# One scratch operand of a float64 split moves from SBUF to a PSUM bank

## The chip, the cores and the metric
One Trainium2 chip, one of its cores. The metric is the device time of one execution in microseconds (us). Engines: TensorE multiplies matrices, VectorE and ScalarE work elementwise on SBUF and PSUM, GpSimd works elementwise on SBUF and issues the indexed transfers, SyncE issues the other transfers. In the profile they are PE (PEld for its weight loads), DVE, ACT, POOL and SP; a name with a trailing q (SPq) is the engine's instruction queue.

## The reference
Three layers, one after the other: a gated recurrent attention (4 x 8 heads, 768 positions, 40 wide), a mixture of 8 experts with one expert per token (3072 tokens of 320), and a dense layer with a rational function between its two products.

```
for t in range(S): C = f*C + i*v k^T;  n = f*n + i*k;  y[t] = sigmoid(o) * (C q) / max(|n q|, 1)
idx = argmax(xn @ en.T / tau);  gate_w = softmax(...)[idx]
for e in range(8):
    h = max(x[mask] @ w1[e], 0);  out[mask] = gate_w[mask] * (h @ w2[e])
h = x @ w_in;  g = (a0 + a1 h + a2 h^2 + a3 h^3) / (1 + |b0||h| + |b1|h^2 + 1e-6);  out = g @ w_out
```

Products are made from a high and a low part of each operand, three products for one, to keep float32 accuracy. `w_in` and `w_out` arrive as float64; the kernel sees each number as two 32-bit words and builds its high and low part itself.

## The kernel before
The program is written out in full: every engine's instructions stand in a fixed order, and an instruction starts when the semaphores it waits for have come.

The change lies in the expert stage, from about 225 to 465 us of the profiled execution. Its loop (line 1665) runs over n = 0 to 65; n = 8e + fb stands for expert e and one 128-wide block of its 1024 hidden columns. A step n issues `gemm1(n)` (line 1460: eight matmuls at line 228 into one of two PSUM banks `ph`, after which ScalarE writes `hh`, line 1469, and VectorE `hl`, line 1470) and `gemm2(n-2)` (lines 1484 to 1486, into the banks `yb`). At its last block an expert's result is scaled (`ysb`, lines 1498 on VectorE and 1502 on ScalarE) and scattered by GpSimd (line 129). Beside this a step carries, in this order of issue:

- `w_load` (lines 162 to 168, SyncE): the next weights, into two buffers `r`, free again when GpSimd has made the low parts from them;
- `x_load` (line 1436, GpSimd) at an expert's first step, and `x_prep` (transposes at line 1107 on TensorE into `pt`, line 1083 on ScalarE, `xl`/`xr` at line 1088 on VectorE) at its steps 4 to 6;
- `w_hi` and `w_lo` (lines 183, 185 on ScalarE; 192, 196 on GpSimd, with a few of the first on VectorE): high and low parts of the weights;
- steps of `gates` (the softmax weights; its scratch lies in columns 384 to 511 of `vown`) and of the float64 split, interleaved.

The float64 split is `dbl_split(i)` (line 1371), 32 parts: 16 of `w_in` (384 columns) and 16 of `w_out` (320). Each has eight steps, spread over n = 8 to 62 by `dbl_steps`, twice as densely up to n = 40. ScalarE first shifts the exponent (line 1386) into `ct`; then VectorE takes six instructions: the shift and mask (1388), the merge with the sign (1390), the low 9 bits (1393), their sum with the low word (1395), the exponent (1397), the low part (1406). The raw words come by `dbl_load` (lines 1357, 1358, 1361, SyncE) into two buffers `raw`, the load of part i + 1 issued within part i. `vown` is a PSUM bank that only VectorE uses (line 1655); the scratch `st_` lies there for the first 30 parts and in SBUF for the last two (lines 1379 to 1382).

Of the kernel before, what the change touches and what calls it, by code (L numbers as in the profile page):

```python
# [14 lines left out]
ALU = mybir.AluOpType  # L15
# [6 lines left out]
def kernel(  # L22
# [330 lines left out]
    with actx:  # L353
# [24 lines left out]
        for _ in range(12):  # L378
# [11 lines left out]
            out=bmask, in_=bmask, compare_op=ALU.is_ge, fill=0.0, base=0,  # L390
# [3 lines left out]
            out=bmask, in_=bmask, compare_op=ALU.is_ge, fill=0.0, base=D - 1,  # L394
# [512 lines left out]
        for g in range(3):  # L907
# [4 lines left out]
            out=grpf, in0=grpf, in1=cend.unsqueeze(1).broadcast_to([NH, B * 3, NCH]), op=ALU.mult  # L912
# [125 lines left out]
        out=mall, in0=macc.unsqueeze(1).broadcast_to([128, NE, JS, NE]),  # L1038
        in1=perm.unsqueeze(2).broadcast_to([128, NE, JS, NE]), op=ALU.mult,
# [299 lines left out]
    with ExitStack() as mctx:  # L1339
# [26 lines left out]
        def dbl_steps(n):  # L1366

            a, c = (W0 * min(max(v - NFB, 0), 4 * NFB) + W1 * max(min(v, DE) - 5 * NFB, 0) for v in (n, NB))
            return a * ND * NS // c

        def dbl_split(i):

            n = 384 if i < 16 else DM
            raw = sx["raw", i]
            lo32, hi32 = raw[:, 0:n, 0], raw[:, 0:n, 1]
            c = mp.tile([128, 384], I32, name="ct", bufs=2)[:, 0:n]
            cf = c.bitcast(F32)

            if (i + 1) * NS <= dbl_steps(S3N[0]):
                st_ = vown[:, 0:n].bitcast(I32)  # L1380
            else:
                st_ = mp.tile([128, 384], I32, name="st_", bufs=1)[:, 0:n]
            vt = mp.tile([128, 384], F32, name="vt", bufs=1)[:, 0:n]
            ts, stt = nc.vector.tensor_scalar, nc.vector.scalar_tensor_tensor

            nc.scalar.activation(out=cf, in_=hi32.bitcast(F32), func=AF.Abs, scale=2.0**-112)
            yield
            ts(out=c, in0=c, scalar1=3, scalar2=-4096, op0=ALU.logical_shift_left, op1=ALU.bitwise_and)  # L1388
            yield
            stt(out=c, in0=hi32, scalar=-(2**31), in1=c, op0=ALU.bitwise_and, op1=ALU.bitwise_or)  # L1390
            yield

            ts(out=st_, in0=hi32, scalar1=511, scalar2=None, op0=ALU.bitwise_and)  # L1393
            yield
            stt(out=vt, in0=lo32.bitcast(U32), scalar=2.0**-32, in1=st_, op0=ALU.mult, op1=ALU.add)  # L1395
            yield
            ts(out=st_, in0=c, scalar1=-(2**23), scalar2=None, op0=ALU.bitwise_and)  # L1397
            yield
            if i < 16:
                cs = slice(i * 128, (i + 1) * 128)  # L1400
                lo = winl[:, :, cs]
                sv, vv = (x.rearrange("p (k f) -> p k f", k=3) for x in (st_, vt))
            else:
                lo = wsl.tile([128, DM], F32R, name="lo3", tag="hp", bufs=2)
                sv, vv = st_, vt
            stt(out=lo, in0=vv, scalar=2.0**-20, in1=sv.bitcast(F32), op0=ALU.mult, op1=ALU.mult)
            yield
            if i < 16:
                nc.scalar.activation(out=winh[:, :, cs], in_=cf.rearrange("p (k f) -> p k f", k=3), func=AF.Copy)
            else:  # L1410
                r = slice((i - 16) * 128, (i - 15) * 128)
                nc.sync.dma_start(out=wouth_d[r, :], in_=cf)
                nc.sync.dma_start(out=woutl_d[r, :], in_=lo.bitcast(F32))
            yield

        def dbl():
            for i in range(ND):
                for k, _ in enumerate(dbl_split(i)):
                    if k == 0 and i + 1 < ND:
                        dbl_load(i + 1)  # L1420
                    yield
# [136 lines left out]
        with tc.tile_pool(name="ov", bufs=1) as ov, tc.tile_pool(name="ovp", bufs=1, space=PSUM) as ovp:  # L1558
            total = nc.values_load(cnt_i[:, NE:NE + 1], min_val=0, max_val=NT)
            with tc.If(total > 0):  # L1560
# [20 lines left out]
                for e in range(NE):  # L1581
                    n_e = nc.values_load(nt_i[:, e:e + 1], min_val=0, max_val=NTILE)
                    with tc.If(n_e > 0):
# [3 lines left out]
                            out=mk, in0=ekey, scalar1=float(NE - e), scalar2=-(2.0**20), op0=ALU.is_equal, op1=ALU.mult  # L1587
# [6 lines left out]
                        for t in range(NTILE):  # L1594
                            nc.gpsimd.indirect_dma_start(
                                out=over[:, :], out_offset=bass.IndirectOffsetOnAxis(ap=idx[:, t:t + 1], axis=0),
# [5 lines left out]
                            out=mk, in0=tokf, scalar1=past[:, e:e + 1], scalar2=2.0**20, op0=ALU.is_ge, op1=ALU.mult  # L1602
# [6 lines left out]
                        with tc.For_i(0, n_e, 1) as t:  # L1609
# [3 lines left out]
                                out=xo, out_offset=None, in_=x_rows[:, :],  # L1613
# [21 lines left out]
                            for _ in gates(ov, go, xo[:, 0:XI].unsqueeze(1), "o"):  # L1635
# [3 lines left out]
                                out=yo[:, 1:], in0=py, scalar1=go, scalar2=None, op0=ALU.mult  # L1639
                            )  # L1640
                            nc.gpsimd.indirect_dma_start(
                                out=y_sorted[:, :], out_offset=bass.IndirectOffsetOnAxis(ap=ix[:, 1:2], axis=0),
# [22 lines left out]
        for n in range(NB + LAG2):  # L1665
# [30 lines left out]
            if n == 2:  # L1696
# [5 lines left out]
                    out=t4, in0=t4, scalar=2.0**20, in1=slot, op0=ALU.mult, op1=ALU.add  # L1702
# [148 lines left out]
```

## Time and profile before
| | us |
|---|---|
| Median of three runs (lowest, highest) | 845.82 (844.59, 848.88) |
| Profiled execution | 846.1 |
| its span on the core | 844.4 |
| TensorE busy | 773.9 (92%) |
| VectorE busy | 738.0 (87%) |
| ScalarE busy | 490.1 (58%) |
| GpSimd busy | 583.9 (69%) |

The profile is one execution. Its span runs from the first to the last instruction; the execution is 1.7 us longer than that. A matmul's end is modelled, so a busy TensorE is not one at its peak. "The granted clock" is the share of TensorE's full clock that the chip granted in a stretch. A wait is put down to the instruction that came last before the waiting one could start; an instruction that is started but cannot proceed shows no wait, only a longer duration.

### The profile page before, as it was taken

How to read it: one execution, taken by the hardware profiler on the slowest of the kernel's cores; microseconds unless marked ns; L12 is line 12 of the kernel's file. 1: busy time of each engine (PE TensorE's matmuls, PEld its weight loads, DVE VectorE, ACT ScalarE, POOL GpSimd, SP SyncE). 2: the span in 40 equal slices, each digit the busy share in tenths (PEclk: the TensorE clock that was granted, in tenths of full speed). 3: DMA queues.
4: the chain of work that ended last, by engine and by line, in shares of the span. 5: the costliest groups of instructions: out<-in, count | busy, mean ns of one | idle time of the engine just before them, and what ended most of it. 6: DMA issues, size and time to landing. Idle time of an engine off the chain costs nothing.

```text
span 844.4 us, 14448 instructions
## 1 busy us (share of the span) xinstructions
PE 773.9 (92%) x4724; PEld 720.2 (85%) x4724; DVE 738.0 (87%) x1421; ACT 490.1 (58%) x839; POOL 583.9 (69%) x595
## 2 busy tenths in 40 slices
PE   8989898988798997989879899999999999999994
PEld 5877776877697886879879799999999999999993
DVE  7999999997589999889887988888889888988882
ACT  5333333333256554444435787878787877787772
POOL 7554343463475866649664578998989898989883
PEclk7899999888899998989999899999999999999998
DMA  8988787642465766668665303010101010000000
GB/s 209 260 240 240 215 241 222 194 137 82 140 173 172 210 185 184 196 189 240 213 201 186 102 16 110 17 32 16 32 15 33 9 40 9 17 1 24 1 24 24
DMA packets 86964, 102.42 MB, mean 121 GB/s; under 512 B 7915, under 2 KB 79219, under 8 KB 86880
## 3 DMA queue, kind: packets, MB, share of 16 engines
q1 hardware_dynamic: 82976, 88.63, 36.1%
q0 software_dynamic: 3904, 12.77, 4.8%
q8 instruction: 40, 0.66, 0.3%
q14 instruction: 44, 0.36, 0.1%
HBM read 84.01 MB, written 17.93 MB: 121 GB/s over the span
## 4 chain that ended last, share of the span: by engine, by line
PE 48%; DVE 15%; issue 3%; ACT 2%; DMA 2%; POOL 1%; SPq 1%; POOLq 0%; DVEq 0%; ACTq 0%
PE h L228 21%; PE yb L1304 6%; PE yb L1306 6%; PE yb L1305 6%; PE ph L228 4%; DVE ct L1388 3%; DVE ct L1390 2%; DVE hl L1470 2%; DMA raw<-in_w_in 1%; DVE vown L1393 1%; DVE vown L1397 1%; DVE vt L1395 1%; PE yb L1484 1%; PE yb L1485 1%; PE yb L1486 1%
## 5 line engine op out<-in xcount | busy, mean ns | idle before, releaser
L1244 POOL TENSOR_TENSOR U<-U,A 128x768 f32<-128x768 f32 (+1 forms) x65 | 119.3, 1835 | 30.8 <-ACT U L1236 26.1
L1306 PE MATMUL yb<-wo,gl 128*128 128x320 f32 x384 | 119.5, 311 | 1.8 <-POOL gl L1290 1.7
L1304 PE MATMUL yb<-wo,gh 128*128 128x320 f32 x384 | 119.3, 311 | 1.2 <-ACT gh L1287 1.2
L1290 POOL TENSOR_TENSOR gl<-P,gh 128x768 fp32r<-128x768 f32 x63 | 117.8, 1871 | 3.6 <-ACT gh L1287 2.9
L1305 PE MATMUL yb<-wo,gh 128*128 128x320 f32 x384 | 119.0, 310 | 0.0
L1220 ACT ACTIVATE P<-h,coef 128x768 f32<-128x768 f32 (+1 forms) x65 | 64.0, 984 | 72.8 <-PE h L228 72.8
L192 POOL TENSOR_TENSOR l<-r,h 128x384 fp32r<-128x384 f32 x64 | 64.4, 1029 | 49.4 <-ACT h L183 44.5
L228 PE MATMUL h<-xh,winh 128*128 128x384 f32 x256 | 90.9, 355 | 3.9 <-DVE P L1253 3.8
L228 PE MATMUL h<-xl,winh 128*128 128x384 f32 x256 | 86.8, 339 | 0.0
L228 PE MATMUL h<-xh,winl 128*128 128x384 f32 x256 | 86.7, 339 | 0.0
L1248 DVE TENSOR_TENSOR P<-P,h 128x768 f32<-128x768 f32 (+1 forms) x65 | 61.2, 941 | 28.7 <-ACT A L1228 24.0
L1306 PEld LDWEIGHTS yb<-wo,gl 128*128 128x128 f32 x384 | 72.5, 189 | 2.6 <-POOL gl L1290 2.6
L1304 PEld LDWEIGHTS yb<-wo,gh 128*128 128x128 f32 x384 | 72.7, 189 | 1.5 <-ACT gh L1287 1.5
L1305 PEld LDWEIGHTS yb<-wo,gh 128*128 128x128 f32 x384 | 72.7, 189 | 0.0
L1484 PE MATMUL yb<-h,hh 128*128 128x320 f32 (+1 forms) x216 | 68.1, 315 | 2.6 <-DVE ysb L1498 2.6
L1238 POOL TENSOR_SCALAR U<-A,coef 128x768 f32<-128x768 f32 x56 | 55.0, 983 | 21.5 <-ACT A L1228 20.8
L228 PE MATMUL ph<-xh,h 128*128 128x256 f32 (+4 forms) x152 | 57.6, 379 | 11.3 <-DVE hl L1470 6.4
L1485 PE MATMUL yb<-l,hh 128*128 128x320 f32 (+1 forms) x216 | 67.7, 313 | 0.0
L1486 PE MATMUL yb<-h,hl 128*128 128x320 f32 (+1 forms) x216 | 67.6, 313 | 0.0
L1253 DVE SCALAR_TENSOR_TENSOR P<-P,coef,h 128x768 f32<-128x768 f32 (+1 forms) x65 | 65.2, 1002 | 2.3
L196 POOL TENSOR_TENSOR l<-r,h 128x320 fp32r<-128x320 f32 x56 | 48.4, 887 | 23.6 <-ACT h L185 23.5
L1279 DVE SCALAR_TENSOR_TENSOR P<-P,coef,s 128x768 f32<-128x768 f32 (+1 forms) x62 | 62.0, 999 | 1.7
(592 smaller groups left out, 2384.9 us busy)
## 6 DMA issues: line engine op xcount, KB each, us to landing
fb<-fz_d SPq DMA_DIRECT2D x22, 512.0 KB
r<-in_w SPq DMA_DIRECT2D x32, 320.0 KB
r<-in_w SPq DMA_DIRECT2D x32, 256.0 KB
raw<-in_w_out SPq DMA_DIRECT2D x16, 320.0 KB
r<-in_w SPq DMA_DIRECT2D x64, 64.0 KB
raw<-in_w_in SPq DMA_DIRECT2D x32, 128.0 KB
x_rows<-xt SPq DMA_DIRECT2D x24, 164.5 KB
xt<-y_sorted SPq DMA_DIRECT2D x8, 481.5 KB
```

The costliest lines, as they stand in the source:

```text
L192: eng.tensor_tensor(out=l1[:, :, sl], in0=r1[:, :, sl], in1=h1[:, :, sl].bitcast(F32), op=ALU.subtract)
L228: mms = [nc.tensor.matmul(ps, lhsT=a, rhs=b, start=(i == 0), stop=(i == 7)) for i, (a, b) in enumerate(seq)]
L1220: r = nc.scalar.activation(out=part("P", m, i), in_=part("ph", m, i), func=AF.Identity, scale=coef[:, 3:4], bias=coef[:, 2:3])
L1244: eng.tensor_tensor(out=U, in0=U, in1=part("A", m, i), op=ALU.mult)
L1253: r = nc.vector.scalar_tensor_tensor(out=P, in0=P, scalar=coef[:, 1:2], in1=part("ph", m, i), op0=ALU.add, op1=ALU.mult)
L1290: eng.tensor_tensor(out=part("gl", m, i), in0=part("P", m, i), in1=part("gh", m, i).bitcast(F32), op=ALU.subtract)
L1304: nc.tensor.matmul(y, lhsT=gh[:, i, t], rhs=wh, start=first, stop=False)
L1305: nc.tensor.matmul(y, lhsT=gh[:, i, t], rhs=wl, start=False, stop=False)
L1306: nc.tensor.matmul(y, lhsT=gl[:, i, t], rhs=wh, start=False, stop=last)
L1484: nc.tensor.matmul(y, lhsT=hh[:, js], rhs=h2[:, half, :], start=(fb == 0), stop=False)
L1485: nc.tensor.matmul(y, lhsT=hh[:, js], rhs=l2[:, half, :], start=False, stop=False)
L1486: nc.tensor.matmul(y, lhsT=hl[:, js], rhs=h2[:, half, :], start=False, stop=(fb == NFB - 1))
```

## The change
Line 1388 writes its shifted and masked words into `st_` instead of back into `ct`, and line 1390 takes them from there. For the first 30 parts `st_` is `vown`, so 1388 has its output in PSUM and 1390 one of its inputs; for the last two parts `st_` is in SBUF as before.

```
-            ts(out=c, in0=c, scalar1=3, scalar2=-4096, op0=ALU.logical_shift_left, op1=ALU.bitwise_and)
+            ts(out=st_, in0=c, scalar1=3, scalar2=-4096, op0=ALU.logical_shift_left, op1=ALU.bitwise_and)
             yield
-            stt(out=c, in0=hi32, scalar=-(2**31), in1=c, op0=ALU.bitwise_and, op1=ALU.bitwise_or)
+            stt(out=c, in0=hi32, scalar=-(2**31), in1=st_, op0=ALU.bitwise_and, op1=ALU.bitwise_or)
```

No engine has an instruction more or less, and their order is the same on all five. What differs is on VectorE: operands, and the semaphores that it waits for. First VectorE in the middle of expert 2's preparation, part 3 of the split (`ct`, `raw`, `vown`, `vt` as above; DVE_49 is a wait for an earlier VectorE instruction, Activation_49 for ScalarE, DMAHW for a landed transfer).

```order
 L1088 TENSOR_TENSOR xl_4759<-pt,xh_4758 128x512 [waits Activation_49]
 L1072 RECIPROCAL gate<-vown 128x4
-L1388 TENSOR_SCALAR ct<-ct 128x384 [waits Activation_49]
-L1390 SCALAR_TENSOR_TENSOR ct<-raw,ct 128x384 [waits DMAHW6_49,DMAHW5_49,DMAHW7_49,DMAHW4_49,DVE_49]
-L1393 TENSOR_SCALAR vown<-raw 128x384
+L1388 TENSOR_SCALAR vown<-ct 128x384 [waits DVE_49,Activation_49]
+L1390 SCALAR_TENSOR_TENSOR ct<-raw,vown 128x384 [waits DMAHW6_49,DMAHW5_49,DMAHW7_49,DMAHW4_49,DVE_49]
+L1393 TENSOR_SCALAR vown<-raw 128x384 [waits DVE_49]
 L1395 SCALAR_TENSOR_TENSOR vt<-raw,vown 128x384 [waits DVE_49]
 L1470 SCALAR_TENSOR_TENSOR hl<-ph_119,hh 128x512 [waits Activation_49]
```

1388 and 1393 now also wait for the VectorE instruction that used `vown` before them; over the whole program 50 such waits come and 6 go. Then VectorE in expert 5, a part of `w_out`, at the place where line 1388 took longest.

```order
 L1064 TENSOR_TENSOR head<-head,vown 128x3x8 [waits DVE_49]
 L1068 TENSOR_REDUCE vown<-head 128x3 [waits Activation_49]
-L1388 TENSOR_SCALAR ct<-ct 128x320 [waits DMAHW3_49,Activation_49]
+L1388 TENSOR_SCALAR vown<-ct 128x320 [waits DVE_49,Activation_49]
 L1070 TENSOR_SCALAR vown<-vown 128x3 [waits DVE_49]
 L1470 SCALAR_TENSOR_TENSOR hl<-ph_118,hh 128x384 [waits Activation_49]
 L1088 TENSOR_TENSOR xl_6453<-pt,xh_6452 128x352 [waits Activation_49]
 L1072 RECIPROCAL gate<-vown 128x3 [waits DVE_49]
-L1390 SCALAR_TENSOR_TENSOR ct<-raw,ct 128x320 [waits DMAHW5_49]
+L1390 SCALAR_TENSOR_TENSOR ct<-raw,vown 128x320 [waits DMAHW5_49,DMAHW3_49]
```

Here `hl` and `xl`, for which TensorE waits, stand two and three instructions behind line 1388, and nothing is moved. The wait for the earlier transfer out of `ct` (DMAHW3) passes from 1388 to 1390.

## Rows read from the trace of the kernel before

**Rows 1.** The page: span, busy time by engine, the last chain by line.
```profile
span 844.4 us, 14448 instructions
PE 773.9 (92%) x4724; PEld 720.2 (85%) x4724; DVE 738.0 (87%) x1421; ACT 490.1 (58%) x839; POOL 583.9 (69%) x595
...
PE h L228 21%; PE yb L1304 6%; PE yb L1306 6%; PE yb L1305 6%; PE ph L228 4%; DVE ct L1388 3%; DVE ct L1390 2%; DVE hl L1470 2%; DMA raw<-in_w_in 1%; DVE vown L1393 1%; DVE vown L1397 1%; DVE vt L1395 1%; PE yb L1484 1%; PE yb L1485 1%; PE yb L1486 1%
```

**Rows 2.** Busy time by engine in four stretches (length, then us busy).
```profile
core 0: us, PE busy (x) PEld busy (x) DVE busy (x) ACT busy (x) POOL busy (x), PEclk, DMA share, GB/s
242.44:345.86 103.42, 93.33 (x506) 82.98 (x505) 95.90 (x204) 53.81 (x103) 68.47 (x76) 0.95 0.65 189
275.28:309.59 34.31, 31.69 (x174) 27.54 (x173) 33.03 (x71) 18.46 (x35) 23.98 (x27) 1.00 0.65 191
345.86:439.72 93.86, 80.19 (x468) 77.14 (x466) 82.66 (x172) 40.88 (x82) 65.24 (x75) 0.93 0.71 212
403.51:408.16 4.65, 4.65 (x21) 4.61 (x21) 3.56 (x9) 1.58 (x3) 1.85 (x3) 0.63 0.36 122
```

**Rows 3.** TensorE's waits, 242 to 440 us (us in total, times, longest).
```profile
PE pt L1107 <- DVE xl L1088: 14.7, 4, 5.0
...
PE ph L228 <- DVE hl L1470: 6.4, 2, 3.9
...
PE yb L1484 <- DVE ysb L1498: 2.6, 2, 1.7
```

**Rows 4.** Lines 1388, 1390, 1395, 1397: duration in ns, min/median/max.
```profile
L1388 DVE TENSOR_SCALAR ct<-ct x32: 318/391/7395, 247.2 to 459.6; 128x384 int32<-128x384 int32 x16, 128x320 int32<-128x320 int32 x16
...
L1390 DVE SCALAR_TENSOR_TENSOR ct<-raw,ct x32: 455/557/5567, 247.7 to 460.5; 128x384 int32<-128x384 int32 x16, 128x320 int32<-128x320 int32 x16
...
L1395 DVE SCALAR_TENSOR_TENSOR vt<-raw,vown x30: 469/545/556, 249.0 to 442.5; 128x384 f32<-128x384 uint32 x16, 128x320 f32<-128x320 uint32 x14
L1397 DVE TENSOR_SCALAR vown<-ct x30: 483/549/562, 253.3 to 443.0; 128x384 int32<-128x384 int32 x16, 128x320 int32<-128x320 int32 x14
```

**Rows 5.** Timeline at the longest instance of line 1388 (start, duration).
```profile
395.10 7.39 DVE L1388 TENSOR_SCALAR ct<-ct 128x320 int32<-128x320 int32 x1 [0.20 <-ACT ct L1386]
...
400.38 1.93 POOL L192 TENSOR_TENSOR l<-r,h 128x384 fp32r<-128x384 f32 x2
...
402.95 0.51 DVE L1088 TENSOR_TENSOR xl<-pt,xh 128x352 fp32r<-128x352 f32 x1
...
403.51 0.53 PE L1107 MATMUL pt<-ident,xt 128*128 128x128 f32 x3 [4.00 <-DVE xl L1088]
```

**Rows 6.** Line 1388 alone in two of the stretches: VectorE busy, count.
```profile
242.44:345.86 103.42, 14.10 (x17) 0.95 0.65 189
345.86:439.72 93.86, 24.01 (x13) 0.93 0.71 212
```

**Rows 7.** Line 1390 alone in the same stretches.
```profile
242.44:345.86 103.42, 12.92 (x17) 0.95 0.65 189
345.86:439.72 93.86, 11.60 (x12) 0.93 0.71 212
```

**Rows 8.** VectorE's timeline at 268 us, with and without waits on itself.
```profile
267.86 0.55 DVE L1393 TENSOR_SCALAR vown<-raw 128x384 int32<-128x384 int32 x1
268.45 0.55 DVE L1395 SCALAR_TENSOR_TENSOR vt<-raw,vown 128x384 f32<-128x384 uint32 x1
268.92 0.68 DVE L1470 SCALAR_TENSOR_TENSOR hl<-ph,hh 128x512 fp32r<-128x512 f32 x1
...
271.18 0.35 DVE L1388 TENSOR_SCALAR ct<-ct 128x384 int32<-128x384 int32 x1
```

**Rows 9.** Waits of ScalarE's line 1386, 242 to 440 us.
```profile
ACT ct L1386 <- DMA raw<-in_w_in: 10.3, 4, 4.5
...
ACT ct L1386 <- DMA raw<-in_w_out: 5.3, 5, 1.9
ACT ct L1386 <- DVE tbg L1798: 4.5, 1, 4.5
```

**Rows 10.** The longest wait of SyncE's queue in the same stretch.
```profile
SPq L168 <- POOL l L196: 15.3, 4, 5.1
```

## The prediction, made before the run
> **What bounds the kernel now.** I read the page first, then busy time by stretch, then TensorE's waits, then the durations of the changed lines, and last the timeline at the worst of them. The page has TensorE busy for 92% of the span, but two elementwise VectorE lines, 1388 and 1390, hold 3% and 2% of the chain that ended last [rows 1]; these are the two lines that the change edits. Both lie in the expert stage. I cut that into A, 242.44 to 345.86 us (experts 1 to 3, when the split runs densely), and B, 345.86 to 439.72 us (experts 4 to 6) [rows 2]. In A VectorE is busy 95.90 of 103.42 us and is all but full; in B 82.66 of 93.86. TensorE stands still for 14.7 + 6.4 + 2.6 = 23.7 us over both, and every one of these waits ends with a VectorE instruction (`xl`, `hl`, `ysb`) [rows 3].
>
> Why VectorE is late then is seen in durations, not in waits. Line 1388 takes 0.32 us at the least and 7.4 us at the most, line 1390 0.46 and 5.6; lines 1395 and 1397, the same operations on the same tiles but with one operand in `vown`, never exceed 0.56 in 30 instances each [rows 4]. The longest 1388 starts at 395.10 us and ends at 402.49, 0.2 us after GpSimd's last of several adjoining subtractions ends at 400.38 + 1.93 = 402.31; `xl` follows at 402.95 and TensorE restarts at 403.51 after 4.00 us [rows 5]. So a VectorE instruction with all its tensors in SBUF is held until GpSimd pauses, and one with a PSUM operand is not.
>
> **What the change removes.** For 30 parts the two lines get a PSUM operand. For 1388 I take the duration of 1397, the same tensor_scalar from `ct` to `vown`: 0.55 us at 384 columns, 0.49 at 320. For 1390 that of 1395, which also reads `raw` and `vown`: the same two figures [rows 4]. In A stand 17 of each, one of them 320 wide: 16 x 0.55 + 0.49 = 9.3 us each, against 14.10 and 12.92 [rows 6, 7], so VectorE loses 4.8 + 3.6 = 8.4 us of work. In B, all 320 wide: 13 x 0.49 = 6.4 against 24.01 and 12 x 0.49 = 5.9 against 11.60, so it loses 17.6 + 5.7 = 23.3.
>
> **What it adds.** Unheld, 1388 took 0.35 us at 384 columns [rows 8] and 0.32 at 320 [rows 4]; it gets 0.2 and 0.17 us slower. That is already in the sums above. Second, VectorE waits for itself more often: net 26 more waits in A, 18 in B, by the order of instructions. An instruction that waits for the one ahead starts 0.59 us after it (267.86 to 268.45), one that doesn't 0.47 (268.45 to 268.92), so such a wait costs 0.12 us [rows 8]: 3.1 us in A, 2.2 in B. Some waits were there for other reasons, so the bounds are 0 and these. Queued behind each such wait on VectorE is the next `hl` or `xl`, for which TensorE waits; the full 0.12 is what I take.
>
> [...]
>
> **The sum.** A is then limited by VectorE: 95.90 - 8.4 = 87.5 us of work. Its fullest third, expert 2, has 33.03 busy of 34.31 us, 96.3% [rows 2]; packed like that it is 90.9 us, with the waits 94.0. Gain 9.4 us. TensorE's own floor lies lower: 93.33 us busy at a mean granted clock of 0.95 are 88.7 at the full clock, which bounds the gain in A at 14.7.
>
> B is limited by TensorE: VectorE needs only (82.66 - 23.3) / 0.963 + 2.2 = 63.8 us, GpSimd 65.24 busy. [...] With the standstills gone I count 80.19 x 0.93 = 74.6 us. Gain 19.3.
>
> Together 28.7 us. What is late next: the raw words. ScalarE's line 1386, ahead of `hh` in its queue, waits 10.3 + 5.3 = 15.6 us for them; the first, 4.5 us, lies ahead of the held stretches, which leaves 11.1 [rows 9]. These waits now lie beside VectorE's held time and beside work that TensorE has left in its other `ph` bank. How much comes to light is not in the trace; the bounds are 0 and 11.1, and having no nearer row I take the middle, 5.5. Net 23.2 us. The profiled execution's 846.1 becomes 822.9; it stands 0.3 above the median, so the forecast is 822.6. No other stage holds a changed instruction: I count the last two parts, the attention and the dense layer at nothing.
>
> **Rivals.** *The raw loads take VectorE's place.* SyncE's queue waits 15.3 us in four places for GpSimd to free a weight buffer (line 168) [rows 10], with the next raw load queued behind it; GpSimd's bursts at each expert's start don't shrink. If all of the 11.1 us and also line 1386's 4.5 us behind a VectorE instruction [rows 9] come onto the path, the gain is 28.7 - 15.6 = 13.1 and the time 832.7. For it: 0.71 of the DMA engines' time is used in B [rows 2] and the stage must move the same bytes faster. Against it: the sum of ScalarE's waits is below the 23.7 us of VectorE's, and in A its load is only 53.81 of 103.42 us, so it catches up.
>
> *The hold isn't lifted.* 1388 still reads `ct` and 1390 `raw` from SBUF, and if the input decided, the time would stay at 845.8. Against it stand 60 instances of 1395 and 1397 with just such an input, none held [rows 4].
>
> *Slower.* The held stretches might be only where VectorE happens to stand while TensorE is late for GpSimd's low parts of the weights, which come at the end of the same bursts. Then no standstill goes, and A, where VectorE is full, pays 17 x 0.2 + 3.1 = 6.5 us: 852.3. It decides from the point where TensorE's restart follows GpSimd's end rather than VectorE's `xl`. Rows 5 speak against it: `xl` lies between the two, and it is queued behind 1388.
>
> [...]
>
> **How the numbers follow.** The forecast has 0.80, the raw loads 0.13, the hold that stays 0.04, slower 0.03. The forecast's own range runs from 814 (A at TensorE's floor, little of the raw waits: 14.7 + 19.3 - 2) to 831 (the middle of the way to the first rival and some of A's packing lost). With that rival's 832.7 the range for 8 in 10 is 814 to 834. Faster and slower count from 0.5%, 4.2 us, about what a measurement of this kernel tells from no change: 0.93, 0.04 and 0.03.
>
> **What would show it.** In the changed profile lines 1388 and 1390 never exceed 0.6 us in the first 30 parts; TensorE's waits for `xl`, `hl` and `ysb` fall from 23.7 us to under 8; the granted clock over B rises from 0.93 to 0.97 or more; the same steps take about 174 us instead of 197; line 1386's waits for raw words grow. It would be wrong if the two lines are still held, if another VectorE line becomes long where they were, or if TensorE's waits only change their name to `hh`.

## The result and the profile after
| | before | after |
|---|---|---|
| Median, us (lowest to highest, runs) | 846.39 (844.59 to 848.88, 4) | 823.41 (822.94 to 828.62, 4) |
| Profiled execution, us | 846.1 | 823.25 |
| its span, us | 844.4 | 821.2 |

The ratio of the times is 0.974 with a 95% interval of [0.9694, 0.9787]; the forecast was 822.6, in 814 to 834. Two further comparisons of the same two kernels, each against fresh runs of before, gave 0.9781 [0.9738, 0.9823] (826.88 against 845.83) and 0.9739 [0.9715, 0.9763] (824.50 against 846.61). By these medians the change is worth 19 to 23 us.

The page of the kernel after, beside [rows 1]: VectorE's busy time fell by 24.4 us. Line 1388 is no longer among the lines named in the chain that ended last, and 1390 is down to 1%; the loads of weights (`r`) and GpSimd's low parts (line 192) have come in, and the raw words of `w_in` hold 1% as before.

```profile
span 821.2 us, 14468 instructions
...
PE 760.3 (93%) x4724; PEld 707.2 (86%) x4724; DVE 713.6 (87%) x1421; ACT 488.8 (60%) x839; POOL 584.3 (71%) x595
...
PE h L228 21%; PE yb L1306 6%; PE yb L1304 6%; PE yb L1305 6%; PE ph L228 4%; DMA r<-in_w 2%; POOL l L192 1%; DVE hl L1470 1%; PE yb L1484 1%; PE yb L1486 1%; PE yb L1485 1%; PE h L1107 1%; DVE ct L1390 1%; DMA raw<-in_w_in 1%; DVE vown L1393 1%
```

Busy time by engine in the kernel after, in the same steps as [rows 2]: A (steps 8 to 31), B (32 to 55), then expert 7 (56 to 62) and the stretch ahead of the first expert. Columns as there: length, then PE, PEld, DVE, ACT, POOL, clock, DMA share, GB/s.

```profile
239.17:335.55 96.38, 90.66 (x506) 80.41 (x505) 89.55 (x203) 54.12 (x103) 67.00 (x77) 1.00 0.69 203
335.55:412.19 76.64, 75.18 (x467) 71.76 (x465) 61.06 (x172) 38.19 (x77) 61.96 (x71) 1.00 0.80 240
412.19:441.60 29.41, 26.74 (x160) 26.44 (x161) 21.27 (x51) 14.38 (x27) 13.90 (x16) 0.94 0.67 216
0.00:221.15 221.15, 189.49 (x1241) 159.35 (x1242) 206.17 (x609) 84.40 (x226) 117.15 (x208) 0.92 0.75 208
```

The last two in the kernel before, which [rows 2] does not have:

```profile
0.00:225.18 225.18, 196.34 (x1241) 164.92 (x1242) 205.01 (x609) 85.08 (x226) 114.20 (x208) 0.90 0.72 204
439.72:464.63 24.91, 24.91 (x162) 24.80 (x161) 20.15 (x50) 12.58 (x24) 11.94 (x13) 1.00 0.60 190
```

A went from 103.42 to 96.38 us and B from 93.86 to 76.64, with the granted clock at 1.00 in both (0.95 and 0.93 before). Expert 7 went the other way, from 24.91 to 29.41. The attention, ahead of the experts and the same code in both, happened to take 4.0 us less in this execution.

TensorE's waits for VectorE over A and B of the kernel after, for [rows 3], and ScalarE's for the raw words, for [rows 9] (us in total, times, longest):

```profile
ACT ct L1386 <- DMA raw<-in_w_out: 17.4, 8, 4.2
...
ACT ct L1386 <- DMA raw<-in_w_in: 11.3, 7, 4.7
...
PE pt L1107 <- DVE xl L1088: 2.2, 3, 0.9
PE ph L228 <- DVE hl L1470: 2.0, 2, 1.7
...
PE yb L1484 <- DVE hl L1470: 1.4, 1, 1.4
...
PE yb L1484 <- DVE ysb L1498: 0.8, 1, 0.8
```

TensorE's 23.7 us of waits are 2.2 + 2.0 + 1.4 + 0.8 = 6.4; one more, of 0.4 us, ends where expert 7 starts. ScalarE's waits for raw words grew from 15.6 to 28.7 us. The two changed lines in the kernel after, over the first 30 parts, for [rows 4]:

```profile
L1388 DVE TENSOR_SCALAR vown<-ct x30: 495/561/563, 244.1 to 416.5; 128x384 int32<-128x384 int32 x16, 128x320 int32<-128x320 int32 x14
...
L1390 DVE SCALAR_TENSOR_TENSOR ct<-raw,vown x30: 457/553/555, 244.9 to 417.1; 128x384 int32<-128x384 int32 x16, 128x320 int32<-128x320 int32 x14
```

The longest is 0.56 us, where it was 7.4. And the timeline at the place of [rows 5]:

```profile
379.46 1.72 POOL L196 TENSOR_TENSOR l<-r,h 128x320 fp32r<-128x320 f32 x2
...
380.40 0.50 DVE L1388 TENSOR_SCALAR vown<-ct 128x320 int32<-128x320 int32 x1 [0.19 <-issue]
...
381.13 2.00 POOL L192 TENSOR_TENSOR l<-r,h 128x384 fp32r<-128x384 f32 x2
...
381.89 0.53 DVE L1088 TENSOR_TENSOR xl<-pt,xh 128x352 fp32r<-128x352 f32 x1
```

Line 1388 now takes 0.50 us in the middle of a GpSimd subtraction that runs from 379.46 to 381.18, and `xl` follows 1 us later while the next one is under way.

### The profile page after: what moved, and what is told of

It reads as the page before. It is cut to its first block, busy times and chain, and to the rows that moved or that the text cites. A ratio compares the mean times of both kernels' runs of the same rounds, so it can differ in the third digit from the quotient of the medians.

```text
span 821.2 us, 14468 instructions
## 1 busy us (share of the span) xinstructions
PE 760.3 (93%) x4724; PEld 707.2 (86%) x4724; DVE 713.6 (87%) x1421; ACT 488.8 (60%) x839; POOL 584.3 (71%) x595
## 4 chain that ended last, share of the span: by engine, by line
PE 49%; DVE 9%; issue 5%; POOL 4%; DMA 2%; ACT 2%; SPq 1%; POOLq 0%; DVEq 0%; ACTq 0%
PE h L228 21%; PE yb L1306 6%; PE yb L1304 6%; PE yb L1305 6%; PE ph L228 4%; DMA r<-in_w 2%; POOL l L192 1%; DVE hl L1470 1%; PE yb L1484 1%; PE yb L1486 1%; PE yb L1485 1%; PE h L1107 1%; DVE ct L1390 1%; DMA raw<-in_w_in 1%; DVE vown L1393 1%
## 5 line engine op out<-in xcount | busy, mean ns | idle before, releaser
L1248 DVE TENSOR_TENSOR P<-P,h 128x768 f32<-128x768 f32 (+1 forms) x65 | 61.2, 942 | 27.9 <-ACT A L1228 23.2
L228 PE MATMUL ph<-xh,h 128*128 128x256 f32 (+4 forms) x152 | 55.4, 364 | 10.0 <-DVE hl L1470 5.1
L1271 DVE SCALAR_TENSOR_TENSOR U<-U,s 128x768 f32<-128x768 f32 (+1 forms) x62 | 58.0, 935 | 4.8 <-ACT s L1267 4.6
```

Source lines behind the costliest of these rows:

```text
L228: mms = [nc.tensor.matmul(ps, lhsT=a, rhs=b, start=(i == 0), stop=(i == 7)) for i, (a, b) in enumerate(seq)]
```

## The experiments
Stage lengths are read from the profiles as above and say more than totals: over the 14 profiles of all kernels the unchanged stretch up to the first expert took 221.15 to 227.48 us.

| kernel | attention | A | B | expert 7 |
|---|---|---|---|---|
| before | 225.18 | 103.42 | 93.86 | 24.91 |
| after, three profiles | 221.15, 227.48, 222.27 | 96.38, 96.02, 96.00 | 76.64, 76.02, 76.29 | 29.41, 28.79, 28.99 |
| e1: scratch in SBUF | 225.07 | 101.09 | 93.85 | 24.92 |
| e2: change in the first 17 parts | 224.09 | 96.01 | 95.83 | 24.92 |
| e3: change in the others | 225.86 | 102.26 | 77.04 | 29.28 |
| e5: unused instructions of four kinds | 223.82 | 109.47 | 88.30 | 24.91 |
| e6: unused instruction of one kind | 224.65 | 117.82 | 94.29 | 24.92 |
| e9: low parts ahead of indexed transfers | 221.30 | 94.92 | 76.30 | 28.00 |
| e10: only the scatters later | 223.13 | 95.98 | 75.12 | 27.54 |
| e11: e10 and a later load of y | 223.91 | 96.00 | 75.28 | 26.62 |
| e12: e9 and a later load of y, two profiles | 226.12, 221.75 | 94.92, 94.96 | 76.71, 75.03 | 27.08, 27.97 |

**Is it the PSUM bank, or that the words are no longer shifted in place?** The same two lines with their scratch in SBUF (`vt`, which line 1395 overwrites later):

```
-            ts(out=st_, in0=c, ...)
+            ts(out=vt.bitcast(I32), in0=c, ...)
...
-            stt(out=c, in0=hi32, ..., in1=st_, ...)
+            stt(out=c, in0=hi32, ..., in1=vt.bitcast(I32), ...)
```

> Line 1388 writes into a scratch of its own and 1390 reads it from there, as in the changed kernel, but the scratch is in SBUF (vt, which is free at that point). Theory of the hold (a VectorE instruction with all tensors in SBUF stands until GpSimd pauses): the gain is gone, 846 to 850 us, and lines 1388 and 1390 again reach 4 us and more. Rival (the gain came from not working in place, or from the changed semaphore waits): 823 us as in the changed kernel, both lines below 0.6 us.

Measured: 843.45 us against 843.88, ratio 0.9991 [0.9962, 1.0021]: nothing is gained. The durations in this kernel (ns, min/median/max):

```profile
L1388 DVE TENSOR_SCALAR vt<-ct x32: 319/375/7423, 247.7 to 457.8; 128x384 int32<-128x384 int32 x16, 128x320 int32<-128x320 int32 x16
...
L1390 DVE SCALAR_TENSOR_TENSOR ct<-raw,vt x32: 456/558/5765, 248.2 to 458.6; 128x384 int32<-128x384 int32 x16, 128x320 int32<-128x320 int32 x16
```

Both are held as in the kernel before. A tile of its own frees neither line; the scratch in PSUM freed both (0.56 us at the most). The changed waits of VectorE on itself are tested only in part, since in this kernel they come at line 1388 and not at 1393.

**Which parts bring it?** The change in the first 17 parts only (those of A), and in the others only (those of B):

```
+            sh = st_ if i < 17 else c      # the other kernel: i >= 17
+            ts(out=sh, in0=c, ...)
...
+            stt(out=c, in0=hi32, ..., in1=sh, ...)
```

> The change for parts 0 to 16 alone (stretch A), parts 17 to 31 as before. Theory of the hold with the two limits of the prediction: only what A gives, about 7 us by the profiles of before and after, so 839 us; the long instances of 1388 and 1390 of experts 4 to 6 stay (up to 7 us). Rival (what A saves is lost again behind it, since TensorE catches up with the weights): no change, 845 to 846.

> The change for parts 17 to 29 alone (stretch B), parts 0 to 16 as before. Theory: B's 17 us less the 4.6 us that expert 7 lost in the changed kernel, so 833 to 834 us; expert 7's lateness is there as in the changed kernel. Rival (the 4.6 us come from TensorE being early by A and B together): B's 17 us in full, 829.

Measured, against the same 843.88: 837.99 us, 0.99 [0.9864, 0.9937], and 831.55 us, 0.9829 [0.9789, 0.9869]; 5.9 and 12.3 us, together 18.2. By their gains (7 and 12.4 us against 0 and 17) both follow the theory and not the rival. Windows of A, B and expert 7, first with the early parts changed, then with the late ones:

```profile
241.16:337.17 96.01, 90.43 (x507) 80.49 (x506) 89.57 (x203) 54.22 (x103) 66.98 (x77) 1.00 0.69 203
337.17:433.00 95.83, 81.50 (x467) 78.39 (x466) 84.24 (x173) 41.19 (x81) 65.12 (x74) 0.91 0.70 212
433.00:457.92 24.92, 24.92 (x163) 24.81 (x161) 20.16 (x50) 12.59 (x24) 11.95 (x13) 1.00 0.54 178
```

```profile
243.30:345.56 102.26, 92.20 (x507) 81.93 (x505) 95.16 (x204) 53.69 (x103) 68.75 (x76) 0.97 0.65 192
345.56:422.60 77.04, 74.88 (x468) 71.90 (x466) 61.09 (x171) 38.41 (x77) 62.22 (x72) 1.00 0.78 240
422.60:451.88 29.28, 26.62 (x162) 26.37 (x161) 19.33 (x50) 14.77 (x27) 13.12 (x16) 0.94 0.66 211
```

Each stage answers to its own parts. Expert 7's loss comes with a fast B alone, whatever A does; and with a slow B the 24.92 stay.

**What decides the hold?** The kernel after, with one more VectorE instruction behind line 1390 of each part, whose result nothing uses; four kinds by i % 4:

```
+            if i % 4 == 0:   ts(out=du, in0=c, ...)                # SBUF -> SBUF
+            elif i % 4 == 1: stt(out=du, in0=hi32, ..., in1=c)     # 2 x SBUF -> SBUF
+            elif i % 4 == 2: stt(out=st_, in0=hi32, ..., in1=c)    # 2 x SBUF -> PSUM
+            else:            ts(out=st_, in0=c, ...)               # SBUF -> PSUM
```

> The changed kernel with one more VectorE instruction per part behind line 1390, its result unused, of four kinds in turn: (0) one input in SBUF, output in SBUF, as the old 1388; (1) two inputs in SBUF, output in SBUF, as the old 1390; (2) two inputs in SBUF, output in PSUM; (3) one input in SBUF, output in PSUM. If the hold comes from what is read and written in SBUF beside the first input: kinds 0 and 1 reach 1.5 us and more, kind 3 never exceeds 0.6. Kind 2 tells two readings apart: it is held if the second SBUF input decides, not held if any PSUM operand frees an instruction. Time 830 to 845 us.

Measured in one profile, the four kinds in that order (846.28 us, just above the range expected):

```profile
L1393 DVE TENSOR_SCALAR vt<-ct x8: 326/360/4752, 248.4 to 430.2; 128x384 int32<-128x384 int32 x4, 128x320 int32<-128x320 int32 x4
...
L1395 DVE SCALAR_TENSOR_TENSOR vt<-raw,ct x8: 491/558/6010, 256.2 to 440.1; 128x384 int32<-128x384 int32 x4, 128x320 int32<-128x320 int32 x4
...
L1397 DVE SCALAR_TENSOR_TENSOR vown<-raw,ct x7: 499/568/944, 262.3 to 413.1; 128x384 int32<-128x384 int32 x4, 128x320 int32<-128x320 int32 x3
...
L1399 DVE TENSOR_SCALAR vown<-ct x7: 494/561/561, 268.3 to 422.1; 128x384 int32<-128x384 int32 x4, 128x320 int32<-128x320 int32 x3
```

The first two are held and the last is not. The third was in doubt: 0.94 us once in seven. So a kernel with that kind in every part:

```
+            stt(out=st_, in0=hi32, scalar=-(2**31), in1=c, ...)    # 2 x SBUF -> PSUM, result unused
```

> The changed kernel with one more merge per part, two inputs in SBUF and the output in PSUM, its result unused. If the second SBUF input decides the hold, several of the 30 reach 1.5 us and more; if a PSUM operand of any kind frees an instruction, none exceeds 0.6 us (the one of 0.94 us among seven in the probe before then needs another cause). Time 830 to 848 us by the one, 828 to 834 by the other.

Measured in one profile, the added line and a long instance beside GpSimd. The time, 861.24 us, lies 13 us above the range expected: the added line makes A 21 us and B 18 us longer than after the change.

```profile
L1391 DVE SCALAR_TENSOR_TENSOR vown<-raw,ct x30: 499/568/6049, 249.1 to 453.9; 128x384 int32<-128x384 int32 x16, 128x320 int32<-128x320 int32 x14
```

```profile
335.54 6.04 DVE L1391 SCALAR_TENSOR_TENSOR vown<-raw,ct 128x384 int32<-128x384 int32 x1
335.92 1.71 POOL L196 TENSOR_TENSOR l<-r,h 128x320 fp32r<-128x320 f32 x2
337.58 1.94 POOL L192 TENSOR_TENSOR l<-r,h 128x384 fp32r<-128x384 f32 x2
339.49 1.66 POOL L196 TENSOR_TENSOR l<-r,h 128x320 fp32r<-128x320 f32 x2
```

It is held until 341.58, 0.4 us after GpSimd's adjoining run ends at 341.15, though its output lies in PSUM. So any PSUM operand is not enough: with two inputs in SBUF the instruction was held where it writes SBUF (up to 6.01 us) and where it writes PSUM (up to 6.05). For line 1390 the input taken from PSUM decides: 5.6 us at the most without it, 0.56 with it. Line 1388 has one input; it was held when it writes SBUF, for up to 7.4 us, and not when it writes PSUM, 0.56 at the most. That is five kinds, three held and two not; why the place of these operands decides is not shown.

**Why does expert 7 lose 4 us?** SyncE's queue in the kernel after, ahead of expert 7, which starts at 412.19:

```profile
400.42 1.16 SPq L166 DMA_DIRECT2D r<-in_w  x2
405.58 0.40 SPq L168 DMA_DIRECT2D r<-in_w  x1
...
407.87 1.67 SPq L1112 DMA_DIRECT2D xt<-y_sorted  x1
409.82 0.39 SPq L162 DMA_DIRECT2D r<-in_w  x1
```

The same transfers in the kernel before, where expert 7 starts at 439.72:

```profile
420.47 1.17 SPq L166 DMA_DIRECT2D r<-in_w  x2
425.83 0.40 SPq L168 DMA_DIRECT2D r<-in_w  x1
...
428.12 0.37 SPq L1112 DMA_DIRECT2D xt<-y_sorted  x1
428.76 0.39 SPq L162 DMA_DIRECT2D r<-in_w  x1
```

The weight load that stood 11.0 us ahead of expert 7 now stands 2.4 us ahead (3.4 in the two later profiles of the change). Line 168 stands for 4.0 us, up to 405.58, until GpSimd frees a buffer; that is not new, it stood for 4.2 us up to 425.83 before. New is that TensorE reaches expert 7 so soon behind it. In the kernel after, three scatters (from 400.18) hold GpSimd until 403.80, and the subtraction of line 196 that frees the buffer ends at 405.55. GpSimd, ScalarE and TensorE show both ends of that:

```profile
402.83 0.97 POOL L129 DMA_INDIRECT y_sorted<-ysb,yrow  x1 [0.30 <-issue]
403.83 1.72 POOL L196 TENSOR_TENSOR l<-r,h 128x320 fp32r<-128x320 f32 x2
...
410.49 0.74 ACT L185 ACTIVATE h<-r 128x640 fp32r<-128x640 f32 x1 [3.77 <-DMA r<-in_w]
...
415.30 0.84 ACT L183 ACTIVATE h<-r 128x768 fp32r<-128x768 f32 x1 [3.36 <-DMA r<-in_w]
...
418.05 0.43 PE L228 MATMUL ph<-xh,h 128*128 128x352 f32 x1 [2.67 <-DVE hl L1470]
```

ScalarE waits for the weights at line 183; `hh`, `hl` and TensorE come behind it. TensorE's standstill of 2.67 us is over half of the 4.5 us that expert 7 lost in this profile; from 418.95 on the granted clock is 0.50 for 3.4 us, and TensorE is busy 1.8 us longer than before. In the two later profiles the clock stays at 1.00 and the standstills of expert 7 are 3.5 and 3.7 us.

The transfers are also crowded there. The first 6.8 us of expert 7, before and then after, with the DMA engines' share as the last number but one:

```profile
439.72:446.50 6.78, 6.78 (x48) 6.77 (x47) 6.64 (x18) 4.28 (x11) 4.95 (x6) 1.00 0.47 147
412.19:418.95 6.76, 4.09 (x25) 3.84 (x26) 2.88 (x7) 3.65 (x8) 3.69 (x5) 1.00 0.98 304
```

So two causes are possible: the loads are issued late, or the DMA engines, busy 0.98 of the time, deliver them late.

Four kernels tried the order of issue, each on top of the change. e9 puts GpSimd's low parts ahead of both kinds of indexed transfers; e10 only the scatters behind them; e11 is e10 with the load of y (line 1112, one of SyncE's) a step later; e12 is e9 with that.

```
-                    y_scatter(e, j, ysb)                  # e9, e10, e11, e12
+                    late.append((e, j, ysb))              # issued behind w_lo of the step
...
-            if n == NB - 12:                              # e11, e12
+            if n == NB - 11:
                 y_load(0)
...
-            if fb == 0 and 1 < e + 1 < NE:                # e9, e12: moved behind w_lo
-                x_load(e + 1)
```

> The changed kernel with GpSimd's low parts of the weights ahead of its token gathers (first step of an expert) and ahead of its scatters (second step). Theory: expert 7 is late because SyncE's next weight load waits for GpSimd's low parts behind three scatters, so the loads now go out 3 to 5 us earlier, expert 7 takes 25 to 26 us instead of 29.4, and the time is 3 to 5 us below the changed kernel. Rival (the transfers themselves are the limit, 0.80 of the DMA engines busy in B): expert 7 stays at 29 us and the time is the same.

> Only the scatters behind the low parts, the gathers where they were. Theory: the scatters make up most of the wait of line 168, so 2 to 4 us below the changed kernel; rival: as the changed kernel.

Measured, beside the change itself (826.88 us in the same comparison): 822.83, 0.9726 [0.9693, 0.976], and 824.35, 0.9757 [0.9717, 0.9798]; the intervals overlap with the change's. Expert 7 in each:

```profile
410.70:438.70 28.00, 26.00 (x162) 24.74 (x161) 19.66 (x50) 14.53 (x27) 13.67 (x16) 1.00 0.68 214
```

```profile
412.09:439.63 27.54, 25.99 (x162) 24.73 (x161) 19.73 (x50) 14.52 (x27) 13.05 (x14) 1.00 0.68 211
```

Against the three profiles of the change (28.79 to 29.41) that is 0.8 to 1.4 us less and 1.3 to 1.9 us less: a part of the loss, and for e9 a smaller one than was expected. Its SyncE queue shows why: the load of y must wait for the scatters, which are now later, and stands ahead of the next weights; it starts 5.2 us after the transfer ahead of it has been issued.

```profile
407.27 0.37 SPq L1112 DMA_DIRECT2D xt<-y_sorted  x1
407.93 0.39 SPq L162 DMA_DIRECT2D r<-in_w  x1
```

> The scatters behind the low parts as in the run before, and the first load of the dense layer's tokens (line 1112, which waits for all scatters so far) one step later, behind the weight load of its step instead of ahead of it. Theory: expert 7 is late because SyncE's weight loads stand behind two waits, line 168's for GpSimd and line 1112's for the scatters; with both out of the way expert 7 takes 25 to 26 us instead of 27.5, and the time is 1 to 3 us below that run (821 to 823). Rival (the transfers are slow in themselves): expert 7 stays at 27 to 28 us.

> The same with the gathers behind the low parts too. Theory: expert 7 at 25 to 26 us instead of 28.0, stretch A 1 us shorter as before with the gathers moved, 820 to 822 us. Rival: expert 7 at 28.

Measured, against 843.57 us of before: 822.66 us, 0.9748 [0.9703, 0.9792], and 821.38, 0.971 [0.9658, 0.9762]. Expert 7 takes 26.62 us in e11 and 27.08 us in e12, and 27.97 us in e12's second profile; the 25 to 26 us expected of both are not reached.

In e11 expert 7 is 2.2 to 2.8 us shorter than after the change alone, over half of its loss, so the order in the two queues carries a good part of it. The moved load has a price of its own: in both kernels TensorE now waits for the tokens that it brings, 0.7 us in e11, 0.5 and 1.9 us in e12. The wait in e12's second profile:

```profile
PE pt L1107 <- DMA xt<-y_sorted: 1.9, 1, 1.9
```

The rest, 1.0 to 1.7 us, stays open. The DMA engines are still busy for 0.86 of the first 6.8 us of expert 7 in e11 and 0.96 to 0.97 in e12, so the second cause is not ruled out; no kernel here moved fewer bytes. Finally the change twice more, once in the comparison with e9 and e10 and once beside e12 on one chip:

> The changed kernel once more, beside the next two on one chip. By the stages of the profiles so far (A 6 us shorter, B 17, expert 7 4.4 longer) the change is worth 19 us, ratio 0.978; the 4 us by which the profiled attention stage was shorter should not come again, since nothing is changed there. Rival (the attention stage is really faster): ratio 0.973 and attention again near 221 us.

> The last variant again, beside the changed kernel on one chip: by the stages 1 us less in A and 2 us less in expert 7, so 3 us below the changed kernel, ratios 0.971 and 0.975. If the two intervals overlap wholly, the reordering is not shown to be worth anything in the total.

> The changed kernel beside it: ratio 0.974 to 0.978; A 96, B 76 and expert 7 29 us, the attention stage anywhere from 221 to 228 us.

Measured: the change 826.88 us in the earlier comparison (ratio above); on one chip, against 846.61 us of before, e12 822.77, 0.9717 [0.9697, 0.9738], and the change 824.50, 0.9739 [0.9715, 0.9763]. e12 is 1.7 us lower, but the intervals overlap: that it beats the change in total is not shown. The dense layer, behind expert 7, takes 381.1 to 382.2 us in the profiles of e9 and e11 and the first of e12, against 379.6 to 380.1 after the change, so part of the gain may be lost there (not in e10 and the second of e12, which have 379.7 and 380.0). The ratio 0.978 that the stages asked of the change came in the first of its two comparisons. The attention took 227.48 us there and 222.27 in the other, so it is not faster by the change.

## Why the prediction was right, and where it was not
- **The hold and its release: right.** Lines 1388 and 1390 stay at or below 0.56 us, A's 17 of each take 17 times 557 and 550 ns, 9.5 and 9.35 us (9.3 forecast), e1 takes the gain away by moving the scratch back. The rule as the prediction put it, that an instruction with a PSUM operand is not held, is too wide: e6 refutes it for two SBUF inputs (6.05 us with the output in PSUM). It gave the right answer because both edits avoid that case.
- **B: right.** 74.6 us forecast, 76.0 to 76.6 measured; TensorE busy 75.18 at a granted clock of 1.00, as the step "80.19 x 0.93 = 74.6 us" said. That the clock would be full with the standstills gone was the author's estimate. In the three profiles of the change and in e3 B's clock is 1.00; in before, e1 and e2, with the late parts held, it is 0.91 to 0.93. TensorE waits 1.3 us there for VectorE.
- **A: gain too large by about 2 us.** 94.0 forecast, 96.0 to 96.4 measured. The busy term was off: VectorE is busy 89.55 us, not 87.5. Its busy time fell by 6.35 us, not 8.4, although the two lines by themselves lost 8.2 (27.0 to 18.8). Busy time counts overlapping instructions once, and an instruction that waits for the one ahead no longer overlaps it ([rows 8]: 0.08 us of overlap without such a wait). Over A these overlaps fall from 8.1 to 5.4 us, summed from the two traces. So part of the wait's price sat in the busy time. VectorE's idle time came near, 6.8 us against 94.0 - 87.5 = 6.5, but not as it was made up: the packing of 96.3% was expert 2's alone, and all of A was packed to 95.90 / 103.42 = 92.7% before and to 89.55 / 96.38 = 92.9% after. TensorE's 90.66 us are close behind.
- **The raw loads: size not shown.** The 5.5 us were booked in A and B. The two together take 173.0 us (about 174 forecast), so of the gain of 28.7 us, 4.4 are missing there. That this is the raw loads is not shown: A's part is mostly the busy term above, and TensorE's waits in A and B name VectorE but for 0.2 us. ScalarE's waits did grow, from 15.6 to 28.7 us. The argument that ScalarE catches up is not shown either, because the chain that ended last does run through these loads. In B it does so in two of three profiles of the change, for 10.0 and 5.7 us, and not in the kernel before (but for 6.2 us in e1, which is held as before); in A for 5.7, 17.0 and 7.3 us against 11.5 before. B in the second profile of the change, a line that the view cuts off at its end:

```profile
by line: DMA raw<-in_w_out 13.1%; PE ph L228 12.8%; DMA r<-in_w 8.4%; issue 5.3%; PE yb L1484 5.0%; PE yb L1485 4.7%; DVE hl L1470 4.5%; PE yb L1486 4.4%; DVE vown L1388 4.0%; DVE ct L1390 3.8%; DVE vown L1393 3.3%; DVE vown L1397 3.3%; DVE
```

- **Expert 7: put at nothing, and wrong.** The step "No other stage holds a changed instruction" let only the changed lines' own stages change. Expert 7 lost 3.9 to 4.5 us by the weights' loads, through a queue that the prediction named (line 168 behind GpSimd) and counted for the raw words only. A stage with almost no changed line lost what a faster one ahead of it had used up of its lead.
- **The total came so close by luck.** Span 844.4 to 821.2 is 23.2 us, the forecast's figure. Rounded, it is made of 7.0 in A, 17.2 in B, -4.5 in expert 7, -0.8 in expert 0, 0.1 in the dense layer and 4.0 in the attention, which the change does not touch; the attention's 4.0 make up for expert 7. Over A, B and expert 7 alone the three profiles gain 19.8, 21.4 and 20.9 us against the one profile of before. With the lines held as before, A took 101.09 us in e1, 2.3 less than in that profile. So the change is worth 19 to 21 us by its stages, 2 to 4 less than forecast.
- **Rivals.** The hold that stays and the slower kernel are refuted by the durations and by TensorE's waits: they had followed VectorE, not GpSimd's low parts. The first rival was right that supply comes next; it asked 15.6 us, and what came is about 4 in expert 7, by the weights.
- **The price of a VectorE wait on itself**, 0.12 us each, was not measured by itself, and the two lines were not freed one at a time.

## What to carry to other kernels
Look for elementwise instructions whose durations have a far tail while their neighbours' do not: the hold does not show as a wait (line 1388 at its longest had 0.20 us of wait ahead of it and took 7.39 us). Where long VectorE durations end with GpSimd's work, as here, try what freed these two lines: for a two-input operation one input from PSUM (line 1390: 0.56 us at the most instead of 5.6, and no slower for it, 0.55 us against 0.56 unheld), for a one-input operation like line 1388 a PSUM output (0.56 at the most instead of 7.4, at a price of 0.2 us). And when a stage gets faster, ask how far ahead of the next one its transfers are issued in a fixed order: that lead is what shrank here, from 11.0 to 2.4 us.

## What was not expected of the hardware
- A VectorE instruction with its output in PSUM but two inputs in SBUF was held for up to 6.05 us, about as long as one with all three operands in SBUF (6.01).
- In e6 VectorE's instruction did not finish between adjoining GpSimd instructions: the one that starts at 335.54 us stood through three groups of them, 6.04 us, and finished 0.4 us after the last of them ended.
